# Linear attention and a gated feed-forward layer on one core: normed x of one superblock transposed by DMA, weights in three groups, a new order of all steps

## The chip, the cores and the metric

The kernel runs on one core of one Trainium2 chip. The metric is the device time of one execution in microseconds. Before the change three runs took 199.66, 199.82 and 200.43 us; the median is 199.82 us.

## What is computed

```
for t in range(768):                                  # per batch (4) and head (8), head size 48
    cur      = einsum('bhd,bhe->bhde', u * k[t], v[t])
    y[t]     = einsum('bhd,bhde->bhe', r[t], state + cur)
    state    = w[t] * state + einsum('bhd,bhe->bhde', k[t], v[t])
x  = y as 3072 tokens of 384
xn = x / sqrt(mean(x * x) + 1e-6) * rms_g
out = (silu(xn @ w_gate) * (xn @ w_val)) @ w_out      # 384 -> 1536 -> 384
```

r, k, v, w come as (4, 8, 768, 48) in float32, the weights in float32, and the output is (3072, 384) in float32.

## The kernel before

**Tiles.** Time is cut into six superblocks n of 128 steps, each with j = 0 to 3 for the batch: 128 tokens by 384 columns. A step of the program is written `name.n.j`. The recurrence becomes matmuls inside a superblock, with a running state `st` carried from one to the next.

**Attention steps of one tile.** `load_w`, `load_r`, `load_k`, `load_v` bring the inputs through SP's queue. `ln` (ScalarE) takes the logarithm of w, `cs_mm` (TensorE) sums it over time against a triangular mask, `cs_add` (DVE, superblocks 2 and up) makes the second sum, `exp_r` and `exp_k` (ScalarE) take the exponentials. `r_mul` (DVE) and `k_mul` (DVE in superblocks 0 and 1, GpSimd after) scale r and k into the tile `rk`. In superblock 1 the exponentials lie in SBUF (tiles `er`, `ek`), otherwise r's lie in PSUM. `rk` is transposed: by TensorE (`rk_pe`) and a ScalarE copy (`rk_tr`) in superblocks 0 and 1, by DMA from SP's queue (`rk_tr`) after. `q_mm` multiplies the transposed r and k into two PSUM banks; `q_mask_e` (DVE), `q_copy_o` (ScalarE) and `q_mask_o` (GpSimd, in superblock 0 DVE) mask them into `qts`. `cast_v` makes v bf16. `st_mm` and `st_new` make the next state. `bonus_mul` (two GpSimd multiplies, r by k and then by u), `bonus_sum` (DVE) and `bonus_v` (GpSimd) make the u term `ydiag`. `y_mm` puts the attention output in PSUM. `x_add` (DVE) adds `ydiag`; in superblock 0 TensorE adds it instead (`x_pe`).

**Norm.** `x_sq` (ScalarE) sums the squares, `x_rstd` makes the factor (GpSimd; ScalarE in superblock 0), `xn_mul` (ScalarE) writes the normed x in bf16. It is then transposed into `xnt`, in one of two ways. In superblocks 0 to 3: `xn_pe` (three TensorE transposes of 128x128 into one bank) and `xn_out` (DVE, a copy times the gain rms_g). In superblocks 4 and 5: `xn_tr` (a DMA transpose from SP's queue, L590), and after all four tiles `xn_gain`, three multiplies of 128x512 by the gain (L615 on DVE, L612 on ScalarE for one of them in superblock 4).

**Feed-forward.** For each superblock all four tiles go together, 512 tokens. `gate_mm.n.f` and `val_mm.n.f` (f = 0 to 11, L626, three matmuls each) fill two PSUM banks each in turn (rings `a`, tiles ps_au and ps_av, and `b`, ps_bu and ps_bv); `silu` (ScalarE) and `h_mul` (DVE) empty them into `ht`. `o_mm` (L672, twelve matmuls), `o_out` and `out_dma` give the output; they stand in the order when all twelve units of the superblock are done, between the attention steps of the next. `ln` and `exp` use one function table of ScalarE, `silu` another; `act` (L231) loads a table (L233) whenever the next function needs the other.

**Order.** The text ORDER lists every step. The program walks through it and calls the functions, so that each engine and each queue gets its instructions in that order; an engine runs on as far as its data and its place in its own list let it. `warm` steps are TensorE matmuls on zeros that nothing reads; 13 more stand ahead of everything. PSUM banks are dealt out by the same order: a step takes a bank whose last reader stands ahead of it. Weights are fetched on GpSimd's queue, which casts them: `load_gv.g.h` for the gate (h = 0) and value (h = 1) columns of group g, `load_wo` for the output weights. With GV = (0, 4, 12) group 0 holds the units f = 0 to 3 and group 1 the units 4 to 11.

**Start.** Ahead of the listed steps stand constants, a memset of the whole `st` (L313), and two TensorE broadcasts: u to all partitions (L333, copied by L334) and the gain as columns (L336, L337).

## Time and profile before

| what | us |
|---|---|
| median of three runs | 199.82 |
| span of the profiled execution | 199.4 |
| first feed-forward matmul starts | 31.30 |
| last matmul ends | about 196.4 |
| TensorE busy | 194.7 |
| DVE busy | 151.5 |
| ScalarE busy | 137.1 |
| GpSimd busy | 125.7 |

The span is from the first to the last instruction of one execution; the run times were taken in other executions, and their median is 0.42 us more. A row of the timeline gives the start, the duration, the engine, the line, the operation, the tiles and how many neighbouring instructions were merged, and in brackets the idle time of the engine before it with what released it. Matmuls overlap: a unit of three that lasts 0.81 us is followed by the next after 0.65 us.

### The profile page before, as it was taken

The numbers are of one execution on the slowest core, as the hardware profiler recorded it, in microseconds if no ns is written. First come the engines' busy times: TensorE is split into PE (matmuls) and PEld (weight loads), VectorE is DVE, ScalarE is ACT, GpSimd is POOL, SyncE is SP. The second block draws the span as 40 slices with busy tenths as digits, with TensorE's granted clock in tenths as the row PEclk, the third lists the DMA queues.
The fourth block names the chain that finished last, engine by engine and source line by source line (L and its number), as shares of the span: only waits on it lengthen the run. The fifth ranks groups of instructions, "written<-read, shape, count | busy, mean of one in ns | idle before, by whom it ended". The sixth has DMA issues, their size and how long they took to land.

```text
span 199.4 us, 4410 instructions
## 1 busy us (share of the span) xinstructions
PE 194.7 (98%) x1577; PEld 115.6 (58%) x1577; DVE 151.5 (76%) x290; ACT 137.1 (69%) x279; POOL 125.7 (63%) x184
## 2 busy tenths in 40 slices
PE   7999999999999999999999999999999999999994
PEld 3566666465765565665556665556555565555562
DVE  6157999799998799987889989987887873173611
ACT  3279998697998468968659959489886683164300
POOL 5369795099489777899857899967686861000000
PEclk9999999999999999999999999999999999999999
DMA  6999999999989999999989999986399012032012
GB/s 147 265 229 191 169 206 208 201 207 191 203 173 212 204 191 227 217 191 191 177 175 226 214 203 215 179 174 139 122 190 219 0 24 60 2 116 82 0 59 100
DMA packets 121566, 32.41 MB, mean 163 GB/s; under 512 B 116420, under 2 KB 120392, under 8 KB 121544
## 3 DMA queue, kind: packets, MB, share of 16 engines
q1 hardware_dynamic: 119504, 28.58, 67.8%
q0 software_dynamic: 2032, 3.54, 9.9%
q8 instruction: 12, 0.20, 0.4%
q14 instruction: 10, 0.08, 0.1%
q10 hardware_dynamic: 8, 0.00, 0.0%
HBM read 25.96 MB, written 4.72 MB: 154 GB/s over the span
## 4 chain that ended last, share of the span: by engine, by line
PE 88%; DMA 5%; DVE 2%; POOL 2%; issue 1%; ACT 0%
PE ps_bu L626 12%; PE ps_av L626 12%; PE ps_au L626 11%; PE ps_bv L626 11%; PE ps_qu L672 7%; PE ps_qz L672 7%; DMA wg_sb<-in_moe_w_gate_dram 5%; PE ps_qx L672 5%; PE ps_qv L672 5%; PE ps_qz L502 1%; PE ps_qx L552 1%; PE ps_qv L502 1%; PE ps_qv L333 1%; PE ps_qu L285 1%; PE ps_qu L502 1%
## 5 line engine op out<-in xcount | busy, mean ns | idle before, releaser
L672 PEld LDWEIGHTS <-ht 128*128 128x128 bf16 x300 | 28.2, 98 | 16.6
L626 PEld LDWEIGHTS <-wg_sb 128*128 128x128 bf16 x216 | 23.1, 114 | 19.8 <-DMA wg_sb<-in_moe_w_gate_dram 0.9
L626 PEld LDWEIGHTS <-wv_sb 128*128 128x128 bf16 x216 | 23.0, 114 | 18.3
L658 DVE TENSOR_TENSOR ht<-ps_bv,sg 128x512 bf16<-128x512 f32 x35 | 24.0, 687 | 10.2 <-PE ps_bv L626 9.1
L658 DVE TENSOR_TENSOR ht<-ps_bu,sg 128x512 bf16<-128x512 f32 x37 | 25.4, 687 | 6.9 <-PE ps_bu L626 5.8
L235 ACT ACTIVATE sg<-ps_av 128x512 bf16<-128x512 f32 x37 | 22.0, 596 | 12.2 <-PE ps_av L626 11.6
L626 PE MATMUL ps_av<-xnt,wg_sb 128*128 128x512 bf16 x111 | 30.1, 380 | 0.0
L626 PE MATMUL ps_bu<-xnt,wv_sb 128*128 128x512 bf16 x111 | 30.1, 380 | 0.0
L626 PE MATMUL ps_au<-xnt,wg_sb 128*128 128x512 bf16 x105 | 28.5, 380 | 0.5 <-DMA wg_sb<-in_moe_w_gate_dram 0.5
L626 PE MATMUL ps_bv<-xnt,wv_sb 128*128 128x512 bf16 x105 | 28.5, 380 | 0.0
L235 ACT ACTIVATE sg<-ps_au 128x512 bf16<-128x512 f32 x35 | 21.0, 600 | 10.5 <-PE ps_au L626 8.7
L467 POOL TENSOR_TENSOR ruk<-rt,kt 128x384 f32<-128x384 f32 x24 | 24.0, 1001 | 6.1 <-DMA kt<-in_k_dram 5.2
L468 POOL TENSOR_TENSOR ruk<-ruk,u_bc 128x384 f32<-128x384 f32 x24 | 24.7, 1030 | 1.9
L520 POOL TENSOR_SCALAR_AFFINE_SELECT qts<-qts 128x512 bf16<-128x512 bf16 x20 | 12.8, 650 | 15.1 <-ACT qts L513 14.6
L477 POOL TENSOR_TENSOR ydiag<-vt,diag 128x384 f32<-128x384 f32 x24 | 20.2, 843 | 1.7 <-DVE diag L472 1.6
L461 POOL TENSOR_TENSOR rk<-kt,ek 128x384 bf16<-128x384 f32 x16 | 15.9, 1004 | 2.3 <-ACT ek L235 2.3
L672 PE MATMUL ps_qu<-wo_sb,ht 128*128 128x384 bf16 (+1 forms) x96 | 15.0, 306 | 0.0
L672 PE MATMUL ps_qz<-wo_sb,ht 128*128 128x384 bf16 x84 | 14.8, 326 | 0.0
L233 ACT ACT_TABLE_LOAD x10 | 12.8, 1283 | 1.8 <-PEq L709 1.6
L472 DVE TENSOR_REDUCE diag<-ruk 128x8 f32<-128x384 f32 x24 | 13.0, 543 | 0.2 <-POOL ruk L468 0.2
L235 ACT ACTIVATE lw<-wt 128x384 bf16<-128x384 f32 (+1 forms) x20 | 11.1, 577 | 2.6 <-DMA wt<-in_w_dram 2.6
L585 ACT ACTIVATE xn<-xb,rstd 128x384 bf16<-128x384 f32 x20 | 11.8, 603 | 0.8 <-POOL rstd L580 0.7
(180 smaller groups left out, 379.8 us busy)
## 6 DMA issues: line engine op xcount, KB each, us to landing
rt<-in_r_dram SPq DMA_DIRECT2D x24, 192.0 KB, 4.0
kt<-in_k_dram SPq DMA_DIRECT2D x24, 192.0 KB, 4.2
vt<-in_v_dram SPq DMA_DIRECT2D x24, 192.0 KB, 4.0
out_dram<-ob SPq DMA_DIRECT2D x23, 192.0 KB, 2.3
wt<-in_w_dram SPq DMA_DIRECT2D x16, 192.0 KB, 4.0
wt<-in_w_dram SPq DMA_DIRECT2D x4, 384.0 KB, 4.4
wo_sb<-in_moe_w_out_dram POOLq DMA_DIRECT2D x3, 384.0 KB, 7.0
wg_sb<-in_moe_w_gate_dram POOLq DMA_DIRECT2D x1, 768.0 KB, 10.3
```

What stands on the lines that cost most here:

```text
L233: nc.scalar.preload_act_table_set(table_name)
L235: return nc.scalar.activation(**kw).ins
L461: eng.tensor_tensor(out=rk[:, n % 2, j, 1, :, 0:D], in0=inp["k", n, j], in1=bank["cs_k", n, j][:, 0:DM].rearrange("p (h d) -> p h d", h=H) ...
L467: nc.gpsimd.tensor_tensor(out=ruk[n, j], in0=inp["r", n, j], in1=inp["k", n, j], op=ALU.mult)
L468: nc.gpsimd.tensor_tensor(out=ruk[n, j], in0=ruk[n, j], in1=u_bc, op=ALU.mult)
L472: nc.vector.tensor_reduce(out=diag[n, j].rearrange("p h o -> p (h o)"), in_=ruk[n, j], axis=mybir.AxisListType.X, op=ALU.add)
L477: nc.gpsimd.tensor_tensor(out=ydiag[n, j], in0=inp["v", n, j], in1=diag[n, j].to_broadcast([128, H, D]), op=ALU.mult)
L520: nc.gpsimd.affine_select(out=qts[n, j][:, 1], in_=qts[n, j][:, 1], compare_op=ALU.is_gt, fill=0.0, base=0, pattern=[[0, NP], [1, 128]], c ...
L585: nc.scalar.activation(out=xn, in_=xb[n, j], func=AF.Copy, scale=rstd[n, j][:, 1, c:c + 1])
L626: nc.tensor.matmul(ps[:, cols], lhsT=units(ws, c, f), rhs=xnt[n][:, c, cols], start=(first and c == 0), stop=(c == KC - 1))
L658: nc.vector.tensor_tensor(out=ht[n][:, f, :], in0=bank.pop(("v", n, f)), in1=bank.pop(("sg", n, f)), op=ALU.mult)
L672: nc.tensor.matmul(ps[:, cols], lhsT=ht[n][:, f, b * L:(b + 1) * L], rhs=wo_sb[:, f, cols], start=(f == 0), stop=(f == FC - 1))
```

## The change

- X normed in superblock 3 is transposed by four `xn_tr` and multiplied by three `xn_gain`, in place of four `xn_pe` and four `xn_out`. The choice is made by which steps ORDER lists.
- GV = (0, 4, 8, 12): three groups of four units for gate and value, so six `load_gv` of equal size in place of two small and two large ones. They stand in the order 0.0, 0.1, 2.0, 1.0, 1.1, 2.1.
- `cast_v` of superblock 0 moves from ScalarE to GpSimd (CAST_ACT).
- The memset of `st` is dropped.
- The broadcasts of u and of the gain become steps (`u_mm`, `u_out`, `g_mm`, `g_out`). On TensorE they stay at the same place.
- The bonus product multiplies r by u first (`bonus_u`) and then by k.
- ORDER is new throughout. SP's first loads are now k, w, r, w, w, r, w, k, r, v, k, r, k, v, v (tiles 0.1, 0.1, 0.0, 0.0, 0.2, 0.1, 0.3, 0.0, 0.2, 0.0, 0.2, 0.3, 0.3, 0.1, 0.3); `ln.3.0` stands between SiLUs of superblock 1, and the last `y_mm` of superblock 5 directly ahead of the `o_mm` of superblock 4. The count of `warm` steps is 36 as before; one of them now follows the first `gate_mm`.
- PARTS and BEHIND are empty, so the functions that use them (`part`, `landed`) change nothing; `gate_h` and `val_h`, which no step used, are gone.

The core of the diff:

```diff
-    CAST_ACT = sel("00 01 02 03 10 11 12 13")
+    CAST_ACT = sel("10 11 12 13")
...
-    nc.vector.memset(st, 0.0)
...
-    u_ps = psum("q", None, [128, DM])
-    nc.tensor.matmul(u_ps, lhsT=ones_row, rhs=u_row, start=True, stop=True)
-    nc.vector.tensor_copy(out=u_bc.rearrange("p h d -> p (h d)"), in_=u_ps)
...
-    GV = (0, 4, 12)
+    GV = (0, 4, 8, 12)
...
+    def bonus_u(n, j):
+        ruk[n, j] = pt.tile([128, H, D], FP32, name="ruk", bufs=NRUK)
+        nc.gpsimd.tensor_tensor(out=ruk[n, j], in0=inp["r", n, j], in1=u_bc, op=ALU.mult)
+
     def bonus_mul(n, j):
-        ruk[n, j] = pt.tile([128, H, D], FP32, name="ruk", bufs=NRUK)
-        nc.gpsimd.tensor_tensor(out=ruk[n, j], in0=inp["r", n, j], in1=inp["k", n, j], op=ALU.mult)
-        nc.gpsimd.tensor_tensor(out=ruk[n, j], in0=ruk[n, j], in1=u_bc, op=ALU.mult)
+        if (n, j) not in ruk:
+            bonus_u(n, j)
+        nc.gpsimd.tensor_tensor(out=ruk[n, j], in0=ruk[n, j], in1=inp["k", n, j], op=ALU.mult)
```

From ORDER after the change, three places. Before the first `gate_mm`:

```
st_mm.0.3 cast_v.0.2 warm.6.0 warm.20.0 y_mm.0.2 r_mul.1.1 k_mul.1.1 bonus_mul.1.0 x_pe.0.3 y_mm.0.3 x_sq.0.2
x_rstd.0.0 xn_mul.0.0 st_mm.0.0 xn_pe.0.1 warm.15.0 load_gv.2.0 warm.16.0 st_new.0.0 load_gv.1.0 bonus_sum.1.0
...
xn_pe.0.3 warm.33.0 rk_tr.1.0 xn_out.0.3 r_mul.1.3 st_mm.0.1 cs_mm.1.2 exp_r.1.2 exp_k.1.2
bonus_mul.1.3 gate_mm.0.3 bonus_sum.1.1 k_mul.1.3 st_new.0.2 load_gv.2.1 warm.30.0 silu.0.3 val_mm.0.0 gate_mm.0.0
```

The norm of superblock 3:

```
o_mm.2.0 xn_mul.3.1 xn_tr.3.1 out_dma.1.2 x_rstd.3.2 x_sq.3.3 cs_add.4.0 load_r.5.0 st_new.3.3 x_rstd.3.3 exp_r.4.0
cs_mm.4.1 o_mm.2.2 cs_add.4.1 bonus_mul.4.2 exp_r.4.1 xn_mul.3.3 exp_k.4.1 exp_k.4.0 w_tot.4.0 r_mul.4.0 xn_mul.3.2
o_out.2.0 ln.4.2 xn_tr.3.3 xn_tr.3.2 w_tot.4.1 cs_mm.4.3 cs_add.4.3 k_mul.4.0 o_mm.2.1 bonus_sum.4.2 r_mul.4.1
st_mm.4.0 exp_r.4.3 k_mul.4.1 exp_k.4.3 w_tot.4.3 r_mul.4.3 bonus_mul.4.0 cs_mm.4.2 o_out.2.1 o_mm.2.3 cs_add.4.2
o_out.2.2 exp_r.4.2 out_dma.2.0 xn_gain.3.1 xn_gain.3.0 exp_k.4.2 rk_tr.4.1 rk_tr.4.0 k_mul.4.3 w_tot.4.2 xn_gain.3.2
```

The norm of superblock 5:

```
y_mm.5.2 x_rstd.5.1 val_mm.4.11 x_add.5.2 xn_mul.5.1 val_mm.4.6 h_mul.4.11 y_mm.5.3 h_mul.4.6 o_mm.4.3 x_add.5.3
x_sq.5.3 x_rstd.5.3 x_sq.5.2 o_mm.4.0 xn_tr.5.1 xn_tr.5.0 o_out.4.3 out_dma.4.3 x_rstd.5.2 xn_mul.5.3 xn_tr.5.3
xn_mul.5.2 o_mm.4.1 o_mm.4.2 xn_tr.5.2 xn_gain.5.2 xn_gain.5.1 xn_gain.5.0 gate_mm.5.2 val_mm.5.7 val_mm.5.2 o_out.4.1
```

More of the change, by code (lines that the diff above doesn't have):

```diff
@@ L86 @@
-h_mul.2.10 q_mask_o.3.3 bonus_sum.3.3 q_mask_o.3.2 cast_v.3.3 val_mm.2.11 xn_mul.3.0 q_mask_e.3.2 val_mm.2.9 silu.2.8
-h_mul.2.11 y_mm.3.2 st_mm.3.3 y_mm.3.3 load_r.4.2 ln.4.0 bonus_v.3.3 x_add.3.1 load_w.4.2 h_mul.2.9 val_mm.2.8
-x_add.3.3 cs_mm.4.0 bonus_mul.4.1 ln.4.1 cs_mm.4.1 x_sq.3.1 xn_pe.3.0 x_add.3.2 x_sq.3.2 cs_add.4.0 h_mul.2.8
-st_new.3.3 o_mm.2.0 x_sq.3.3 o_mm.2.2 exp_r.4.0 load_k.4.2 cs_add.4.1 exp_k.4.0 r_mul.4.0 x_rstd.3.1 xn_mul.3.1
-o_out.2.0 x_rstd.3.2 xn_mul.3.2 w_tot.4.0 ln.4.2 exp_r.4.1 load_r.5.1 x_rstd.3.3 k_mul.4.0 xn_out.3.0 load_r.4.3
```

272 lines of the change are left out of this document (135 added, 137 removed).

## Prediction, made before the changed kernel was run

> **What bounds the kernel now.** I read the page first, then the busy time by stage, then each engine's rows of the first 42 us. Page:
>
> ```profile
> span 199.4 us, 4410 instructions
> PE 194.7 (98%) x1577; PEld 115.6 (58%) x1577; DVE 151.5 (76%) x290; ACT 137.1 (69%) x279; POOL 125.7 (63%) x184
> ```
>
> Busy time by stage (PE, PEld, DVE, ACT, POOL, clock, DMA share, GB/s), cut where PE's first feed-forward matmul starts, where each superblock's first one starts, and where its last matmul ends:
>
> ```profile
> 31.30:196.43 165.13, 164.65 (x1323) 97.40 (x1320) 129.61 (x245) 114.37 (x230) 102.95 (x151) 1.00 0.75 156
> 196.43:199.39 2.96, 0.00 (x0) 0.00 (x0) 0.00 (x0) 0.32 (x1) 0.00 (x0) 1.00 0.29 102
> 31.30:62.08 30.78, 30.31 (x276) 18.47 (x274) 28.78 (x55) 25.86 (x52) 19.17 (x29) 1.00 1.04 200
> 90.66:119.27 28.61, 28.61 (x250) 17.17 (x248) 25.77 (x51) 21.39 (x44) 23.71 (x35) 1.00 0.98 198
> 146.83:173.05 26.22, 26.22 (x201) 15.05 (x200) 16.22 (x30) 15.27 (x32) 13.94 (x23) 1.00 0.38 77
> ```
>
> From 31.30 to 196.43 TensorE is packed: 0.48 us idle in 165.13, all in the first stage. The clock is full, so nothing off TensorE can shorten this part; it can only open gaps. The one gap, and the start of the part, stand in PE's rows:
>
> ```profile
> 31.30 0.81 PE L626 MATMUL ps_au<-xnt,wg_sb 128*128 128x512 bf16 x3
> 36.92 0.84 PE L626 MATMUL ps_au<-xnt,wg_sb 128*128 128x512 bf16 x3 [0.47 <-DMA wg_sb<-in_moe_w_gate_dram]
> ```
>
> It is the wait for the big second group of gate weights. The time therefore is a sum of four: start 31.30, matmuls 164.65, gaps 0.48, tail 2.96 = 199.39. I change each in turn. The profiled span is 199.4 where the median of the runs is 199.82; I add 0.42 at the end.
>
> **Matmuls.** Four `xn_pe.3` go. One costs PE its step to the next matmul, and the DVE copy `xn_out` goes with it; three `xn_gain` come on DVE:
>
> ```profile
> 27.39 0.33 PE L596 MATMUL ps_qu<-ident,xn 128*128 128x128 bf16 x3
> 27.56 0.33 PE L374 MATMUL ps_qv<-still 128*128 128x384 bf16 x1
> 30.61 0.54 DVE L607 TENSOR_TENSOR xnt<-ps_qv,gT 128x384 bf16<-128x384 bf16 x1
> 169.24 0.88 DVE L615 TENSOR_SCALAR xnt<-xnt,gT 128x512 bf16<-128x512 bf16 x3 [2.82 <-DMA xnt<-xn]
> ```
>
> 4 x 0.17 = 0.68 off PE (27.56 - 27.39). One `warm` of 0.16 now comes after the first `gate_mm`. Everything else after that step is the same set of matmuls: 164.65 - 0.68 + 0.16 = **164.13**. DVE saves 4 x 0.54 - 0.88 = 1.3 us in a stage where it has 2.8 us free (28.61 - 25.77); worth nothing to the end.
>
> **The start.** The first `gate_mm` needs `xn_out.0.3`, the last item of three queues. Removed first: the memset of `st`, and the casts from ScalarE.
>
> ```profile
> 3.25 1.34 DVE L313 MEMSET st<- 128x1536 uint32 x1 [0.27 <-issue]
> 7.00 0.56 DVE L334 COPY u_bc<-ps_qv 128x384 f32<-128x384 f32 x1 [2.41 <-PE ps_qv L333]
> L379 ACT CAST vb<-vt 128x384 bf16<-128x384 f32 x8 | 4.0, 509 | 0.0
> L381 POOL CAST vb<-vt 128x384 bf16<-128x384 f32 x16 | 8.0, 503 | 0.6 <-DMA vt<-in_v_dram 0.6
> ```
>
> The memset ends at 4.6, and DVE then waits 2.4 us for the broadcast of u: nothing gained. ScalarE sheds 4 x 0.51 = 2.0 us, GpSimd takes 4 x 0.50. GpSimd's rows of the start:
>
> ```profile
> 8.21 0.99 POOL L467 TENSOR_TENSOR ruk<-rt,kt 128x384 f32<-128x384 f32 x1 [4.39 <-DMA kt<-in_k_dram]
> 13.82 1.00 POOL L467 TENSOR_TENSOR ruk<-rt,kt 128x384 f32<-128x384 f32 x1 [0.92 <-DMA rt<-in_r_dram]
> 19.76 0.99 POOL L351 DMA_DIRECT2D wg_sb<-in_moe_w_gate_dram  x1
> 25.80 0.81 POOL L351 DMA_DIRECT2D wv_sb<-in_moe_w_val_dram  x1
> L468 POOL TENSOR_TENSOR ruk<-ruk,u_bc 128x384 f32<-128x384 f32 x24 | 24.7, 1030 | 1.9
> L477 POOL TENSOR_TENSOR ydiag<-vt,diag 128x384 f32<-128x384 f32 x24 | 20.2, 843 | 1.7 <-DVE diag L472 1.6
> ```
>
> The first multiply waits for SP's fifth load and the third pair for its tenth: (13.82 - 8.21)/5 = 1.1 us a load. In the new order it wants the sixth (r of 0.1), so it starts at about 9.3; that r comes before k lets the first of two multiplies run early does not change their sum. Up to the last cast GpSimd does four pairs (4 x 2.06), four casts (2.0), four `bonus_v` (3.4) and two weight issues (1.8): 15.4, so 24.7, plus about 0.8 for loads of v now issued later: 25.5. That cast gates `y_mm.0.2`, then the chain on ScalarE:
>
> ```profile
> 25.08 0.47 ACT L570 ACTIVATE junk<-ps_av 128x384 bf16<-128x384 f32 x1
> 28.45 0.58 ACT L585 ACTIVATE xn<-ps_bu,rstd 128x384 bf16<-128x384 f32 x1
> ```
>
> From this square to the last `xn_mul` it took 3.95 us for eight steps; the new queue has eight there too. 25.5 + 0.3 for the matmuls + 3.95 = 29.75. PE still has `xn_pe`, a warm, `st_mm` and `cs_mm.1.2` behind it (1.15): 30.9. So by GpSimd and ScalarE the start stays near 31. DVE decides:
>
> ```profile
> 24.91 1.35 DVE L455 TENSOR_TENSOR rk<-rt,er 128x384 bf16<-128x384 f32 x1
> 26.66 2.18 DVE L455 TENSOR_TENSOR rk<-rt,er 128x384 bf16<-128x384 f32 x1
> L455 DVE TENSOR_TENSOR rk<-rt,er 128x384 bf16<-128x384 f32 x4 | 4.7, 1184 | 0.0
> L461 DVE TENSOR_TENSOR rk<-kt,ek 128x384 bf16<-128x384 f32 x4 | 3.2, 807 | 0.0
> 20.71 0.69 DVE L509 TENSOR_TENSOR qts<-ps_qx,mask_lt 128x512 bf16<-128x512 f32 x1
> ```
>
> Multiplies with both inputs in SBUF (`er`, `ek`) are stretched, up to 2.18, where GpSimd is busy beside them. Ahead of `xn_out.0.3` there were three of them (two r, one k); now four (k of 1.1 too), and `bonus_sum.1.0`. The fourth bonus product leaves GpSimd at 9.3 + 11.7 = 21.0; from there DVE has 4 masks (0.69 each in the row, some 0.6 from start to start: 2.4), 2 sums and `w_tot` (1.0), 2 `st_new` (0.9), 4 `xn_out` (1.9) = 6.2, and the four multiplies. At the means 2 x 1.18 + 2 x 0.81 = 4.0 the queue ends at 31.2; with the two r as in this very stretch (1.35 + 2.18) and k at 0.81, 5.1, at 32.3. Below, PE's own matmuls of the start, 18.29 of 18.45 busy with their fillers, allow no more than about 1.4 off (to 29.9). I take **32.0**: the nearest rows are the two of this stretch.
>
> ```profile
> 12.85:31.30 18.45, 18.29 (x204) 11.86 (x203) 16.63 (x30) 16.85 (x42) 15.84 (x18) 1.00 1.06 194
> ```
>
> [...]
>
> **Gaps.** (a) Weights: six parts of equal size in GpSimd's queue instead of four. The first may stand at about 21.4 (19.76 before), the second at 24 (25.80 before), the third to fifth at 27.6 to 30; the order puts units of groups 1 and 2 after seven units of group 0 and an `rk_pe` (5.0 us), so at about 37. I take 0, with 0.5 as the upper end from the row at 36.92, and to -0.48 against before.
> (b) Between `rk_pe.1.2` and `q_mm.1.2` PE now has two feed-forward units and an `st_mm` (1.5) where it had three units and the `st_mm` (2.1). In that time ScalarE must reach and copy `rkT`:
>
> ```profile
> 62.72 0.65 PE ps_bu L626 x3
> 31.28 1.01 ACT L493 COPY rkT<-ps_qz 128x1024 bf16<-128x1024 bf16 x1
> ```
>
> With one SiLU (0.6) ahead of the copy it is 0.2 late; with none, nothing: 0.2.
> (c) `ln.3.0` now stands among the SiLUs of superblock 1, which adds two table loads:
>
> ```profile
> L233 ACT ACT_TABLE_LOAD x10 | 12.8, 1283 | 1.8 <-PEq L709 1.6
> L235 ACT ACTIVATE sg<-ps_av 128x512 bf16<-128x512 f32 x37 | 22.0, 596 | 12.2 <-PE ps_av L626 11.6
> ```
>
> Load, `ln` (0.5), load, SiLU: 3.7 us after `silu.1.4` until `gate_mm.1.8` gets its bank. From the end of `gate_mm.1.4` PE has five units of 0.65 and four small steps (1.1) before it: 4.35, against 0.8 (until `silu.1.4` is done) + 3.7 = 4.5: 0.2; nothing if ScalarE is early, up to 1 if late.
> (d) Superblock 3 now goes over SP:
>
> ```profile
> L590 SPq DMA_TRANSPOSE xnt<-xn x8: 1177/1200/1605, 134.8 to 166.8; - x8
> xnt<-xn SPq DMA_TRANSPOSE x8, 2.3
> rkT<-rk SPq DMA_TRANSPOSE x16, 3.4
> 165.25 1.95 PE ps_qz L672 x12
> 163.96 0.55 DVE L561 TENSOR_TENSOR xb<-ps_qx,ydiag 128x384 f32<-128x384 f32 x1
> ```
>
> SP issues one in 1.2 us, it lands 2.3 us after. PE covers with four `o_mm` of 1.95 and three small steps, 8.8 us. The last `xn_mul.3.2` stands on ScalarE behind `exp_r.4.1`, which needs `cs_mm.4.1` (6.6 before PE is free) and a DVE add, so it starts 5.8 before; three `exp` and two `xn_mul` follow (0.4 and 0.55 from start to start), so `xn_mul.3.2` ends 3.5 before; 2.3 + 0.88 leave 0.3. But DMA's share there is 0.98, not 0.38 as where the eight ran; with 3.4 it is 0.8 late. The four also hold SP's loads of superblock 5 behind them, which have 5 us and more in hand. I take 0.4.
> (e) Superblock 5: its last `y_mm` moved from before 11 us of PE work to before 7.8 (the four `o_mm`). From `x_add` at 163.96 to the end of the gains at 170.12 the chain took 6.2; a second square, an output copy and the 1.2 us of the transpose ahead are new in it: about 8.0: 0.2.
> Gaps: 0 + 0.2 + 0.2 + 0.4 + 0.2 = **1.0**.
>
> **Sum.** 32.0 + 164.13 + 1.0 + 2.96 (same tail: half-width copy and one output) = 200.1; with 0.42, **200.5**, 0.35% above the median. About 0.5%, 1.0 us, is what a measurement of this kernel tells from no change.
>
> **Rivals.** *Faster:* the order is simply tight everywhere. Start 30.2, gaps 0.1: 30.2 + 164.13 + 0.1 + 2.96 + 0.42 = 197.8. For it: before, hundreds of steps ran with 0.48 of gaps, and ScalarE has 2 us less at the start. Against: GpSimd starts later and has more. *Slower, by the lock:* all four multiplies wait for a GpSimd instruction (r at 2.18 as at 26.66, k at 0.55, an undisturbed pass of this size, plus 1.0: 2 x 2.18 + 2 x 1.55 = 7.5 instead of 5.1): start 32.0 + 2.4 = 34.4, time 202.9; it decides as soon as the four take over 5.5 in sum, because nothing else on DVE gives. For it: GpSimd has no idle time beside them now. Against: the k rows' mean of 0.81. *Slower, superblock 3:* the transposes land behind loads on SP's queue (3.4 plus one load's 1.1 instead of 2.3): 1.7 late instead of 0.4, and 0.4 at superblock 4, whose stage has 2.5 us more GpSimd work by my count of the order: 202.2. For it: the DMA share of 0.98; against: SP stands waiting for `xn_mul.3.1` just before, so that few loads are under way.
>
> **Chances.** Forecast 0.48, its own range 199.3 to 201.8 (start 31.2 to 32.7, gaps 0.6 to 1.6; of it 0.30 within 0.5%, 0.16 above, 0.02 below), faster 0.22, lock 0.15, superblock 3 0.15. So faster 0.24, same 0.30, slower 0.46. The range leaves out the far end of each: 198.0 (faster rival, 197.8, with a little of its gap) to 203.0 (the lock).
>
> **What would show it.** In the new profile: first feed-forward matmul at 32 (30 for the faster rival, 34 for the lock, then with r and k multiplies of over 1.5 us); PE idle 1 us after it, at the places (b) to (e) by name of releaser: DVE `xnt` for superblocks 3 and 5, ACT `sg` for the table loads; 12 table loads. The prediction is wrong if PE shows idle time at a place I do not name, or if its matmul total after the start isn't 0.5 us smaller.

## The result and the profile after

The changed kernel takes 212.83 us (median of four runs, 210.22 to 213.08) where the kernel before takes 199.78. The ratio is 1.0588, 95% interval 1.0518 to 1.0659. Ratios here and below leave out executions that took over 1.5% longer than the fastest of their kernel, which the medians still count, so a ratio can differ from the quotient of two medians. The forecast was 200.5 us with 203.0 as its upper end, so the loss was missed by 12 us. On a second chip the changed kernel, run again unaltered, gave 1.0715 (1.0673 to 1.0756). So a difference of about 1% between runs on different chips says little, and below the stages of the profiles are compared beside the ratios.

The page of the kernel after: span, busy times and the granted TensorE clock in 40 slices.

```profile
span 211.1 us, 4349 instructions
PE 195.1 (92%) x1544; PEld 114.6 (54%) x1565; DVE 148.9 (71%) x288; ACT 140.0 (66%) x277; POOL 128.1 (61%) x190
PEclk9999996999999999999999996999999999999999
```

TensorE's busy time is much as before (194.7), its share fell from 98% to 92%: most of what was added is idle time. Two slices have a lowered clock, at 32 to 37 and at 127 to 132 us. The busy time by stretch (PE, PEld, DVE, ACT, POOL, granted clock, DMA share, GB/s), cut at the steps of the forecast and around those two slices:

```profile
30.14:35.08 4.94, 4.82 (x33) 3.25 (x33) 2.36 (x5) 1.62 (x4) 4.76 (x6) 0.66 1.24 211
36.33:207.70 171.37, 165.69 (x1289) 97.10 (x1308) 128.17 (x242) 117.96 (x232) 101.22 (x149) 0.99 0.72 146
207.70:211.10 3.40, 0.03 (x1) 0.00 (x0) 0.00 (x0) 0.32 (x1) 0.00 (x0) 1.00 0.18 61
124.60:127.06 2.46, 0.19 (x2) 0.00 (x0) 1.70 (x4) 1.10 (x1) 2.38 (x4) 1.00 0.71 190
127.06:131.10 4.04, 3.37 (x12) 1.43 (x14) 2.12 (x5) 1.56 (x3) 2.84 (x3) 0.58 1.14 148
```

The first feed-forward matmul starts at 36.33, the last matmul ends at 207.70. Put against the terms of the forecast (the profiled run itself took 212.78):

| term | forecast | measured | difference |
|---|---|---|---|
| start | 32.0 | 36.33 | +4.3 |
| matmuls and gaps after it | 164.13 + 1.0 | 171.37 | +6.2 |
| tail | 2.96 | 3.40 | +0.4 |
| time minus span | 0.42 | 1.68 | +1.3 |

The last line is no part of the kernel's work: the run times of before exceed its spans by 1.7 us too wherever both come from one execution (202.52 beside a span of 200.8 on the chip of the first experiments); by that, an estimate, the profiled execution of before was some 1.3 us above the median run, which adding 0.42 hid. The two that matter are the start and the gaps.

**The start.** PE's first matmuls of `y_mm.0.2`, which wait for the last cast of v on GpSimd, its first step after its idle stretch, and its first feed-forward unit; then VectorE's rows there:

```profile
25.97 0.36 PE L560 MATMUL ps_av<-vb,qts 128*128 128x48 bf16 x8 [0.76 <-POOL vb L385]
30.14 0.33 PE L604 MATMUL ps_qv<-ident,xn 128*128 128x128 bf16 x3 [1.62 <-ACT rstd L237]
36.33 0.81 PE L634 MATMUL ps_au<-xnt,wg_sb 128*128 128x512 bf16 x2
```

```profile
24.21 0.58 DVE L465 TENSOR_TENSOR rk<-kt,ek 128x384 bf16<-128x384 f32 x1
27.47 0.89 DVE L459 TENSOR_TENSOR rk<-rt,er 128x384 bf16<-128x384 f32 x1 [2.68 <-ACT rstd L237]
28.29 1.34 DVE L465 TENSOR_TENSOR rk<-kt,ek 128x384 bf16<-128x384 f32 x1
29.55 0.54 DVE L545 TENSOR_TENSOR st<-ps_qv,wcol 128x384 bf16<-128x384 f32 x1
33.50 0.56 DVE L615 TENSOR_TENSOR xnt<-ps_qu,gT 128x384 bf16<-128x384 bf16 x1 [1.56 <-PE ps_qu L604]
35.32 0.56 DVE L615 TENSOR_TENSOR xnt<-ps_qx,gT 128x384 bf16<-128x384 bf16 x1 [1.26 <-PE ps_qx L604]
```

VectorE stands for 2.68 us ahead of `r_mul.1.1`. The releaser that is named, a tiny ScalarE step, writes nothing that this multiply reads. Its r is loaded by the later of these two issues on SP:

```profile
L253 SPq DMA_DIRECT2D rt<-in_r_dram x2: 704/984/1264, 19.6 to 20.9; - x2
DMA to landing us min/median/max: 4.0/5.2/6.5
```

Issued at 20.9, landed 6.5 us later: 27.4. (That the longer landing belongs to the later issue is inferred here; a row of the order alone, below, names the load.) Behind the multiply come `k_mul.1.1` and `st_new.0.0` (29.55, L545), and `st_new.0.0` frees the PSUM bank ps_qv that `xn_pe.0.0` needs: PE goes on at 30.14, right after it. PE was idle for 1.62 us, and from here to 35.08 its clock is 0.66 in the mean; one matmul of 128x384 follows another after 0.32 us instead of 0.16. The last two `xn_out` then wait for PE, not PE for them. From 25.97 PE needs 7.04 us for its own list up to the first unit when nothing holds it, as two runs below show: 25.97 + 7.04 + 1.62 of idle time + 1.7 of half rate = 36.33.

**Superblock 3.** SP's rows, then VectorE's gains, then PE:

```profile
120.29 0.53 SPq L690 DMA_DIRECT2D out_dram<-ob  x1
120.87 0.42 SPq L253 DMA_DIRECT2D rt<-in_r_dram  x1
121.38 2.64 SPq L598 DMA_TRANSPOSE xnt<-xn  x2
```

```profile
125.36 1.64 DVE L623 TENSOR_SCALAR xnt<-xnt,gT 128x512 bf16<-128x512 bf16 x2 [1.48 <-DMA xnt<-xn]
127.00 1.08 DVE L623 TENSOR_SCALAR xnt<-xnt,gT 128x512 bf16<-128x512 bf16 x1
```

```profile
127.06 0.41 PE L634 MATMUL ps_av<-xnt,wg_sb 128*128 128x512 bf16 x1 [2.27 <-DVE xnt L623]
128.14 0.59 PE L634 MATMUL ps_av<-xnt,wg_sb 128*128 128x512 bf16 x1 [0.67 <-DVE xnt L623]
128.60 1.47 PE L634 MATMUL ps_au<-xnt,wg_sb 128*128 128x512 bf16 x3
```

The last two transposes are issued at 121.38 and about 122.7, behind an output and a load; the later one lands near 125.3; a gain takes 0.82 and 1.08 us; PE is idle 2.27 us, starts its first unit, waits 0.67 for the third gain, and runs at half rate: a unit lasts 1.47 instead of 0.81. In the profile before, four of VectorE's five gains took 0.35 us; the fifth, one of these two at superblock 4, took 1.09, beside a GpSimd multiply:

```profile
145.22 1.35 DVE L615 TENSOR_SCALAR xnt<-xnt,gT 128x512 bf16<-128x512 bf16 x2
```

**Two smaller places.** An output copy (L682) that waits for an output transfer, which SP issued at 94.28, keeps `h_mul` and with it PE:

```profile
98.71 0.56 DVE L682 COPY ob<-ps_qu 128x384 f32<-128x384 f32 x1 [1.85 <-DMA out_dram<-ob]
100.38 0.81 PE L634 MATMUL ps_bv<-xnt,wv_sb 128*128 128x512 bf16 x3 [0.62 <-DVE ht L660]
155.40 1.96 DVE L623 TENSOR_SCALAR xnt<-xnt,gT 128x512 bf16<-128x512 bf16 x2 [0.31 <-DMA xnt<-xn]
157.41 0.62 PE L634 MATMUL ps_bu<-xnt,wv_sb 128*128 128x512 bf16 x2 [0.81 <-DVE xnt L623]
```

The lower two rows are superblock 4, whose gains are stretched as well. The gaps after the start add up to 171.37 - 164.13 = 7.2 us: 4.4 at superblock 3 (2.4 until its first matmul, 0.9 at the third gain, 1.1 of half rate), 1.3 at superblock 4, 0.8 at 99.6, and some 0.7 in small pieces.

### The profile page after: what moved, and what is told of

Read it like the earlier page. It is cut to its first block, busy times and chain, and to the rows that moved or that the text cites. A ratio compares the mean times of both kernels' runs of the same rounds, so it can differ in the third digit from the quotient of the medians.

```text
span 211.1 us, 4349 instructions
## 1 busy us (share of the span) xinstructions
PE 195.1 (92%) x1544; PEld 114.6 (54%) x1565; DVE 148.9 (71%) x288; ACT 140.0 (66%) x277; POOL 128.1 (61%) x190
## 4 chain that ended last, share of the span: by engine, by line
PE 68%; SPq 8%; DMA 7%; ACT 5%; POOL 5%; DVE 3%; issue 2%; DVEq 0%; ACTq 0%; POOLq 0%
PE ps_au L634 11%; PE ps_bv L634 10%; PE ps_av L634 10%; PE ps_bu L634 9%; SPq L253 6%; PE ps_qx L675 6%; PE ps_qv L675 4%; PE ps_qu L675 3%; PE ps_qz L675 3%; DMA out_dram<-ob 2%; SPq L266 2%; DMA rkT<-rk 2%; DMA rt<-in_r_dram 2%; POOL rk L465 1%; DVE xnt L623 1%
## 5 line engine op out<-in xcount | busy, mean ns | idle before, releaser
L237 ACT ACTIVATE sg<-ps_av 128x512 bf16<-128x512 f32 x35 | 20.9, 598 | 20.1 <-PE ps_av L634 18.4
L660 DVE TENSOR_TENSOR ht<-ps_bu,sg 128x512 bf16<-128x512 f32 x35 | 24.0, 686 | 13.9 <-PE ps_bu L634 8.9
L634 PE MATMUL ps_av<-xnt,wg_sb 128*128 128x512 bf16 x101 | 28.5, 382 | 3.2 <-DVE xnt L623 2.9
L634 PE MATMUL ps_au<-xnt,wg_sb 128*128 128x512 bf16 x109 | 30.6, 387 | 0.3
L660 DVE TENSOR_TENSOR ht<-ps_bv,sg 128x512 bf16<-128x512 f32 x37 | 25.4, 685 | 6.8 <-PE ps_bv L634 3.6
L634 PE MATMUL ps_bu<-xnt,wv_sb 128*128 128x512 bf16 x99 | 28.3, 383 | 1.1 <-DVE xnt L623 0.8
L471 POOL TENSOR_TENSOR ruk<-rt,u_bc 128x384 f32<-128x384 f32 x24 | 24.1, 1003 | 5.6 <-DMA rt<-in_r_dram 5.6
L476 POOL TENSOR_TENSOR ruk<-ruk,kt 128x384 f32<-128x384 f32 x24 | 24.0, 999 | 4.3 <-DMA kt<-in_k_dram 2.6
L675 PE MATMUL ps_qx<-wo_sb,ht 128*128 128x384 bf16 x96 | 16.9, 326 | 0.0
L578 ACT ACTIVATE junk<-xb 128x384 bf16<-128x384 f32 x20 | 10.3, 516 | 5.7 <-DVE xb L569 5.6
L675 PE MATMUL ps_qu<-wo_sb,ht 128*128 128x384 bf16 (+1 forms) x84 | 13.8, 314 | 0.0
```

The costliest lines, as they stand in the source:

```text
L237: return nc.scalar.activation(**kw).ins
L471: nc.gpsimd.tensor_tensor(out=ruk[n, j], in0=inp["r", n, j], in1=u_bc, op=ALU.mult)
L476: nc.gpsimd.tensor_tensor(out=ruk[n, j], in0=ruk[n, j], in1=inp["k", n, j], op=ALU.mult)
L634: nc.tensor.matmul(ps[:, cols], lhsT=units(ws, c, f), rhs=xnt[n][:, c, cols], start=(c == 0), stop=(c == KC - 1))
L660: nc.vector.tensor_tensor(out=ht[n][:, c, cols], in0=bank.pop(("v", n, f))[:, cols], in1=bank.pop(("sg", n, f))[:, cols], op=ALU.mult)
L675: nc.tensor.matmul(ps[:, cols], lhsT=ht[n][:, f, b * L:(b + 1) * L], rhs=wo_sb[:, f, cols], start=(f == 0), stop=(f == FC - 1))
```

## Experiments

The theory after the result had three parts: the late load of r.1.1 holds VectorE, and PE through a bank; the path over DMA costs about 5 us at superblock 3; an idle stretch of PE brings a lowered clock, which doubles its price (1.62 us idle and 1.7 of half rate at the start). The rivals were the lock between VectorE and GpSimd at the start, the gains (not the transposes) at superblock 3, and the new order itself rather than the three named parts. The lock is the prediction's name for a supposition, that a VectorE multiply with both inputs in SBUF waits for a GpSimd instruction to end; shown is that in the profile before the four `r_mul` with both inputs in SBUF took 0.55 to 2.18 us, the two of 1.35 and 2.18 beside GpSimd's work, and the 20 with one input in PSUM 0.54 to 0.56. In the diffs of steps below, a line is a part of ORDER cut to the steps that move.

### The start: the load of r.1.1 earlier

```diff
-warm.1.0 load_r.1.1 rk_pe.0.3
+q_mm.0.1 load_r.1.1 load_k.1.0
```

> The kernel after with one step moved: the load of r for superblock 1, batch 1 is SP's 17th load instead of its 21st. Late-load theory: r_mul.1.1 stood idle 2.68 us on VectorE because this r, issued at 20.9, landed at 27.4; st_new.0.0 behind it held the bank that xn_pe.0.0 needs. With the load early r_mul.1.1 starts at about 24.8, st_new.0.0 at 27.5, TensorE is not idle 1.62 us at 28.5, and the first feed-forward matmul stands at 32.3 to 33 instead of 36.33: 3.3 to 4 us faster, about 209.2. Rival, the VectorE/GpSimd lock of the prediction: the multiplies start earlier but are stretched beside GpSimd (over 1.5 us each), st_new.0.0 still starts at 29, first feed-forward matmul at 35.5 or later: within 1 us of the kernel after.

Measured 215.11 us, ratio 1.0662 (1.0594 to 1.0730); first feed-forward matmul at 35.42. VectorE:

```profile
26.46 2.58 DVE L459 TENSOR_TENSOR rk<-rt,er 128x384 bf16<-128x384 f32 x1
28.97 1.35 DVE L465 TENSOR_TENSOR rk<-kt,ek 128x384 bf16<-128x384 f32 x1
```

The wait is gone, so it had been the load; but the multiply, now beside GpSimd's work (90% busy or more from 26.7 to 32.0 on this run's page), lasts 2.58 instead of 0.89 and ends at 29.04, later than the 28.4 of the changed kernel. The theory that the late load costs the time by itself fell: when the load comes early, the stretched multiply takes its place. The load that moved up also held others back: `r_mul.1.0` waited 1.07 us for its r (0.18 before the move), and `y_mm.0.2` began at 27.72 instead of 25.97. PE is idle there for 0.56 us instead of 1.62 and keeps its clock; less the later `y_mm.0.2`, that is the 0.9 us of the start. Superblock 3 took it back: PE was idle there for 4.51 us, and the clock was low for nearly 7:

```profile
127.00:134.00 7.00, 5.67 (x17) 2.04 (x18) 5.04 (x10) 1.56 (x3) 3.13 (x4) 0.51 0.95 196
```

### The start: both multiplies behind the last xn_out

```diff
-y_mm.0.2 r_mul.1.1 k_mul.1.1 bonus_mul.1.0
+y_mm.0.2 bonus_mul.1.0
...
-xn_out.0.3 r_mul.1.3
+xn_out.0.3 r_mul.1.1 k_mul.1.1 r_mul.1.3
```

> The kernel after with r_mul.1.1 and k_mul.1.1 moved on VectorE from ahead of st_new.0.0 to behind xn_out.0.3; nothing else. Theory after the run with the early load (r_mul.1.1 then started at 26.46 and took 2.58 us, k_mul.1.1 1.35): these two, late for their data or held by GpSimd, are what keeps the bank of st_new.0.0 from xn_pe.0.0. Behind the last xn_out they cost nothing: st_new.0.0 at 27.5 to 28.5, no idle 1.6 us of TensorE, first feed-forward matmul 32.2 to 33.5 (36.33 in the kernel after with half clock, 35.83 in one like it without), the kernel 2.5 to 4 us faster, ratio to before 1.040 to 1.046. Rival: GpSimd's queue (last cast of v at 25.4 to 27, then the chain on ScalarE) sets the start anyway: first matmul at 35 or later, under 1 us won.

Measured 212.73 us, ratio 1.0543 (1.0481 to 1.0604); first feed-forward matmul at 33.29. VectorE, then PE from `y_mm.0.2` on:

```profile
32.76 1.40 DVE L459 TENSOR_TENSOR rk<-rt,er 128x384 bf16<-128x384 f32 x1
34.08 1.35 DVE L465 TENSOR_TENSOR rk<-kt,ek 128x384 bf16<-128x384 f32 x1
```

```profile
26.25 0.36 PE L560 MATMUL ps_av<-vb,qts 128*128 128x48 bf16 x8
38.88 0.81 PE L634 MATMUL ps_bv<-xnt,wv_sb 128*128 128x512 bf16 x3 [0.93 <-DVE ht L660]
```

The idle time ahead of `xn_pe.0.0` is gone and so is the half rate: from 26.25 to 33.29 PE goes through its list in 7.04 us (7.03 in the mended version below). So the two steps ahead of the norm are what made PE stand there. How much that is worth varies: six profiles with the start of the changed kernel unaltered have their first unit at 34.83 to 37.34, so 33.29 is 1.5 to 4.1 us earlier (3.0 against the first of them). But at their new place the multiplies keep `h_mul` of superblock 0, and PE waits 0.93; the stage up to the first `o_mm` took 22.46 instead of 21.38 us. Superblock 3 idled 3.25 us here, and in the median little was won.

### The start: twelve more warm matmuls

```diff
+warm.16.0 warm.40.0 ... warm.51.0 st_new.0.0
```

> The kernel after with twelve more filler matmuls (0.16 us each) on TensorE ahead of xn_pe.0.0, where it stands idle 1.62 us at 28.5. Idle-time theory of the clock: the half clock granted from 30.5 to 35.1 follows from that idle time; filled, the 4.9 us of work after it take about half, the first feed-forward matmul stands at 33.9 and the kernel is 2.4 us faster, about 210.4. Rival: the clock falls for the idle time spread from 10 to 28 us or for something that is not idle time; then nothing changes, or 0.3 us are lost.

Measured 217.02 us, ratio 1.0761 (1.0694 to 1.0829). PE is not idle there and the clock stays full, as the idle-time theory wants, but no time could be won: PE's row of the fillers, three old and twelve new, shows why.

```profile
29.04 5.62 PE L378 MATMUL ps_qx<-still 128*128 128x384 bf16 x15
```

All write one bank and follow each other after 0.36 us, as the three on one bank in the changed kernel do (1.08 in sum at 27.44), not 0.16 as those on changing banks do (7.67, 7.83 and 7.99 there), so `xn_pe.0.0` comes at 34.50, 2.6 us after the bank was free. Inconclusive, by the fault of the experiment.

### Superblock 3: back to TensorE, two ways

```diff
-xn_tr.3.0 ... xn_tr.3.1 ... xn_tr.3.3 xn_tr.3.2 ... xn_gain.3.1 xn_gain.3.0 ... xn_gain.3.2
+h_mul.2.8 xn_pe.3.0 xn_out.3.0 o_mm.2.0
+k_mul.4.0 xn_pe.3.1 xn_out.3.1 o_mm.2.1 xn_pe.3.3 xn_out.3.3 xn_pe.3.2 xn_out.3.2 bonus_sum.4.2 r_mul.4.1
```

> The kernel after with the named part undone alone: superblock 3's normed x goes through TensorE again (xn_pe and xn_out for the four batches, no transposes by DMA and no gains; st_mm.4.0 goes behind them for want of a bank). Theory that the DMA path is what opens the boundary of superblock 3: the 4.4 us lost from the end of the last o_mm of superblock 2 (124.63) on, idle and half clock, go, four times 0.17 of matmuls come back: 3.5 us faster, about 209.3. Rival, that the last xn_mul on ScalarE (ended 121.1) or the new order around it is late anyway: TensorE still stands over 1 us before the first feed-forward matmul of superblock 3 and less than 2 us are won.

Measured 212.07 us, ratio 1.0524 (1.0462 to 1.0586). In this first trial I had put `xn_out.3.3` and `xn_out.3.2` ahead of `r_mul.4.1` on VectorE, and PE waited 1.87 us behind them. The second trial spreads them:

```diff
+h_mul.2.8 xn_pe.3.0 xn_out.3.0 o_mm.2.0
+cs_mm.4.1 xn_pe.3.1 xn_out.3.1 o_mm.2.2
+k_mul.4.0 xn_pe.3.3 xn_out.3.3 o_mm.2.1 xn_pe.3.2 bonus_sum.4.2
+o_out.2.2 xn_out.3.2 exp_r.4.2
```

> The kernel after with superblock 3's normed x on TensorE again, the copies placed on VectorE where their inputs are just ready (in the first trial of this, two of them stood ahead of r_mul.4.1 and made TensorE wait 1.87 us themselves). Theory that the DMA path opens the boundary: TensorE goes from the last o_mm of superblock 2 to the first matmul of superblock 3 with under 0.4 us idle, no half clock there; 4.4 us of loss go, 0.7 of matmuls come back: 3 to 3.7 us faster than the kernel after, ratio to before 1.040 to 1.044. Rival: the last xn_mul or the masks and copies on VectorE are late in this order too: over 1 us idle stays and under 2 us are won.

Measured 208.79 us, ratio 1.0325 (1.0234 to 1.0417), with the last kernel of this study the lowest in the new order, 3.9 us below the run of the moved multiplies on the same chip. From the first `o_mm.2` to superblock 3's first unit:

```profile
115.29:124.85 9.56, 9.54 (x79) 6.10 (x77) 8.94 (x22) 7.37 (x19) 8.07 (x13) 1.00 0.82 192
```

No idle time, clock 1.00; in the changed kernel this stage took 11.19 us (115.87 to 127.06), and the feed-forward behind it 21.09 where it is 19.14 here. That makes 3.6 us for the path over DMA by the stages of these two profiles; by the two ratios, from different chips, it is 5.3.

### Superblock 3: the transposes ahead on SP's queue

```diff
-xn_tr.3.1 out_dma.1.2 x_rstd.3.2 x_sq.3.3 cs_add.4.0 load_r.5.0 st_new.3.3
+xn_tr.3.1 x_rstd.3.2 x_sq.3.3 cs_add.4.0 st_new.3.3
...
-xn_tr.3.3 xn_tr.3.2 w_tot.4.1
+xn_tr.3.3 xn_tr.3.2 out_dma.1.2 load_r.5.0 w_tot.4.1
```

> The kernel after with out_dma.1.2 and load_r.5.0 moved behind the last transpose of superblock 3 on SP's queue. Theory: those two keep the third transpose until 121.38 though its input was ready at 119.9, and the fourth until 122.7. Without them the third goes at 120.3, the fourth at 121.5, the gains start 1.2 us earlier: 1.2 us faster (211.6) if TensorE still falls to half clock, 2.3 us (210.5) if the shorter idle time keeps the clock. Rival: GpSimd's instructions, not the landing, set the end of the gains: under 0.5 us.

Measured 212.97 us, ratio 1.0535 (1.0439 to 1.0632). SP, then VectorE:

```profile
119.72 3.80 SPq L598 DMA_TRANSPOSE xnt<-xn  x3
123.61 0.53 SPq L690 DMA_DIRECT2D out_dram<-ob  x1
```

```profile
125.78 0.56 DVE L682 COPY ob<-ps_qz 128x384 f32<-128x384 f32 x1 [2.58 <-DMA out_dram<-ob]
126.25 1.51 DVE L623 TENSOR_SCALAR xnt<-xnt,gT 128x512 bf16<-128x512 bf16 x2
```

The last two transposes go out some 0.4 us earlier, but now the output transfer is late; VectorE's output copy waits 2.58 us for its buffer, and the gains stand behind that copy. PE was idle 3.25 us. One wait was exchanged for another: what was put behind the transposes became the late one.

### Superblock 3: less GpSimd work beside the gains

This kernel leaves out the bonus products of three tiles, so it does not compute the same output; it serves to see the gains with GpSimd idle.

```diff
+    LEAN = sel("40 43 53")
...
+        if (n, j) in LEAN:
+            nc.gpsimd.tensor_copy(out=ruk[n, j][:, :, 0:1], in_=inp["r", n, j][:, :, 0:1])
+            return
         nc.gpsimd.tensor_tensor(out=ruk[n, j], in0=inp["r", n, j], in1=u_bc, op=ALU.mult)
```

> The kernel after without the two multiplies of the bonus on GpSimd for three blocks (superblock 4, batches 0 and 3; superblock 5, batch 3), and their sums cut to one column: so GpSimd has little or nothing to do while VectorE applies the gains of superblock 3. Lock theory: a gain took 0.82, 0.82 and 1.08 us there because it waited for GpSimd's instruction to end; now 0.35 each, the first feed-forward matmul of superblock 3 comes 0.9 us and the second 1.6 us earlier: 1.6 to 2.5 us faster (with or without the half clock). Rival: the gains are slow because transposes are landing in the same tile or for their own sake: durations unchanged, time within 0.5 us.

Measured 214.10 us, ratio 1.0535 (1.0469 to 1.0602). SP, then VectorE:

```profile
123.46 2.65 SPq L604 DMA_TRANSPOSE xnt<-xn  x2
```

```profile
129.06 0.61 DVE L629 TENSOR_SCALAR xnt<-xnt,gT 128x512 bf16<-128x512 bf16 x2 [3.95 <-DMA xnt<-xn]
129.66 0.34 DVE L629 TENSOR_SCALAR xnt<-xnt,gT 128x512 bf16<-128x512 bf16 x1
```

With GpSimd idle beside them (its last step ended at 126.57) the gains run in 0.34 to 0.35 us from one to the next, where they took 0.82 and 1.08 in the changed kernel beside GpSimd multiplies (one after the other from 122.82 to 129.90): their stretch goes with GpSimd's work, as the lock theory expected. No time was won. In the execution that was profiled (215.50 us) the transposes were issued 2.1 us later than in the changed kernel, 1.0 of it because the whole stage stood later, and took some 4 us to land, so that with the gains cheap the transposes alone made PE wait 3.98 us; whether the other executions went the same way, no profile shows. So the gains need not be the cause for PE to stand, and the rival that they alone are falls.

### The named parts one by one, in the old order

```diff
-    CAST_ACT = sel("00 01 02 03 10 11 12 13")
+    CAST_ACT = sel("10 11 12 13")
```

> The kernel before, its old order kept, with one part of the change: v of superblock 0 cast on GpSimd instead of ScalarE. Theory: GpSimd, which was idle only some 2 us between 12 and 24 us, gets 2.0 us more, its last product for superblock 0 and the casts come up to 2 us later than the matmuls that want them, so the start grows by 0.5 to 2 us: 200.5 to 202. Rival (the prediction's sum: GpSimd's queue with the casts still ends in time): start within 0.3 us, the same time.

```diff
-    GV = (0, 4, 12)
+    GV = (0, 4, 8, 12)
...
-load_gv.0.1 load_gv.1.0 ... bonus_sum.1.1 load_gv.1.1
+load_gv.0.1 load_gv.2.0 load_gv.1.0 ... bonus_sum.1.1 load_gv.2.1 load_gv.1.1
```

> The kernel before with one part of the change: gate and value weights in three groups of four units, the third group issued ahead of the second (its units come first in the old order). Theory: the half-sized parts land earlier, the one wait of 0.47 us for the gate weights at 36.9 goes: 0.3 to 0.5 us faster. Rival: all parts share the same engines, the part that is wanted lands no earlier, and two more issues on GpSimd (0.8 us each) push its products back: the same or up to 0.8 us slower.

```diff
-xn_pe.3.0 ... xn_out.3.0 ... xn_pe.3.1 xn_out.3.1 ... xn_pe.3.3 ... xn_pe.3.2 ... xn_out.3.3 ... xn_out.3.2
+xn_mul.3.0 xn_tr.3.0 ... xn_mul.3.1 xn_tr.3.1 ... xn_mul.3.2 xn_tr.3.2 ... xn_mul.3.3 xn_tr.3.3
+exp_r.4.3 xn_gain.3.1 xn_gain.3.0 xn_gain.3.2 cs_add.4.2
```

> The kernel before, its old order kept, with the named part of the change alone: normed x of superblock 3 transposed by DMA, each transpose right behind its xn_mul in the queues, three gains on VectorE where the last copy stood. Theory: the last xn_mul there ends at 115.5, a transpose takes 1.2 us of SP and 2.3 to 4.2 us to land, and two gains beside a busy GpSimd take 1.6: first feed-forward matmul of superblock 3 at 121 to 123 instead of 119.3, and half clock for 3.4 us after an idle stretch of that length: 2 to 5 us slower. Rival, the prediction's own: 0.4 us late, 0.7 us of matmuls saved: the same time.

The casts alone: 202.36 us, 1.0058 (1.0028 to 1.0088). The three groups alone: 202.44, 1.0046 (1.0011 to 1.0081). The DMA path alone: 208.07, 1.0303 (1.0237 to 1.0369). PE's waits that the first two add, one row of the casts and one of the groups:

```profile
32.73 0.40 PE L484 MATMUL ps_qv<-ident,rk 128*128 128x128 bf16 x4 [0.69 <-DVE rk L461]
```

```profile
42.09 0.84 PE L626 MATMUL ps_bv<-xnt,wv_sb 128*128 128x512 bf16 x3 [1.73 <-DMA wv_sb<-in_moe_w_val_dram]
```

Both are small: a wait just behind the first unit, which itself came no later (31.00, where up to 2 us more were expected), and one for the value weights of the group that now stands third. The DMA path alone, SP, VectorE and PE:

```profile
120.56 1.18 SPq L590 DMA_TRANSPOSE xnt<-xn  x1
```

```profile
123.56 2.43 DVE L615 TENSOR_SCALAR xnt<-xnt,gT 128x512 bf16<-128x512 bf16 x3 [2.15 <-DMA out_dram<-ob]
```

```profile
124.97 0.41 PE L626 MATMUL ps_bv<-xnt,wv_sb 128*128 128x512 bf16 x1 [3.92 <-DVE xnt L615]
```

The same picture as in the changed kernel, in another order of steps: last transpose behind loads and an output, gains of 0.8 us each, 3.92 us of idle time, then half rate (granted clock 0.50 from 126 to 129). (A gain reads no output; the transfer that the row names can't have released it, while the transpose issued at 120.56 lands in about that time, by the 2.3 to 3.0 us that one took in the profile before.) From the first `o_mm.2` to the first `o_mm.3` it took 34.05 us where the kernel before took 27.93, so this is the largest of the named parts, 6 us. (The profiled execution, 209.81 us and the longest of its four, also waited 2.19 and 0.89 us for weights at 35.05 and 39.37, ahead of everything that was changed; that is no cost of the DMA path.)

### The new order without the named parts, and the changed kernel again

```diff
-    CAST_ACT = sel("10 11 12 13")
+    CAST_ACT = sel("00 01 02 03 10 11 12 13")
...
-    GV = (0, 4, 8, 12)
+    GV = (0, 4, 12)
```

with superblock 3 over TensorE as in the second way above.

> The kernel after with all three named parts undone and only the new order of the steps kept: superblock 3 through TensorE (as in the second trial of that), v of superblock 0 cast on ScalarE, weights in two groups. If the parts add up (on the old order alone the casts cost 0.58%, the groups 0.46%, superblock 3 by DMA 3.03%): ratio to before 1.0325 of the second trial less 1.0%, about 1.022, so that the order itself costs some 4.5 us, most of it ahead of the first feed-forward matmul (35.6 in the second trial). Rival, that the order is only as late as the named parts make it: ratio under 1.010, first feed-forward matmul under 32.5.

> The kernel after, unchanged, once more on the chip of this comparison: ratio to before 1.052 to 1.066 as first measured. The half clock should be granted after each stretch of over 1.9 us without a matmul and after none under 1.5 us; the one of 1.6 to 1.8 us before xn_pe.0.0 may go either way.

On one chip: the order alone 209.65 us, 1.0417 (1.0385 to 1.0449); the changed kernel 215.08, 1.0715 (1.0673 to 1.0756). So the order carries somewhat more than half of the loss, and the named parts in it 5.4 us. The expectation, 1.022, was far too low: by the product of their ratios the three parts cost 4.1% in the old order, the new order without them costs 4.2%, and all of it costs 7.2%, so the costs are not a plain sum (the old-order runs are from another chip). "The order" here includes what this run keeps: the dropped memset, the two broadcasts as steps and the bonus product in its new form, which no run tries by themselves. VectorE, PE and the clock at the start of the order alone:

```profile
28.26 0.57 DVE L459 TENSOR_TENSOR rk<-rt,er 128x384 bf16<-128x384 f32 x1 [2.56 <-DMA rt<-in_r_dram]
30.62 0.33 PE L604 MATMUL ps_qv<-ident,xn 128*128 128x128 bf16 x3 [1.76 <-DVE st L545]
36.74 0.81 PE L634 MATMUL ps_au<-xnt,wg_sb 128*128 128x512 bf16 x2
```

```profile
31.00:34.60 3.60, 3.49 (x17) 1.80 (x16) 1.42 (x4) 1.02 (x3) 2.94 (x3) 0.53 1.20 230
```

Without any cast moved and with the old weight groups the start is still 36.74, and here the profile names the load and the step that I had inferred, `st_new` (L545). Stage by stage this kernel's profile (span 208.3) lies 8.9 us above that of before: 5.4 at the start, 1.0 in the feed-forward of superblock 2 (the output copy), 0.7 and 0.9 at the change to superblocks 3 and 4, and under 0.4 anywhere else.

The second profile of the changed kernel (span 211.2) has the same steps and another cause at the start. VectorE waits for no load there; its multiplies are stretched instead, the first two of four:

```profile
22.69 1.68 DVE L459 TENSOR_TENSOR rk<-rt,er 128x384 bf16<-128x384 f32 x1
26.09 1.09 DVE L465 TENSOR_TENSOR rk<-kt,ek 128x384 bf16<-128x384 f32 x1
```

With 1.35 and 1.34 for the other two they sum to 5.46, and `st_new.0.0` begins at 29.64, where with the late load it began at 29.55. PE was idle for 1.07 us, the clock did not fall, and the first unit stands at 34.83. Of the six profiles with this start two show the late load and four the stretched multiplies (5.46 to 5.69 in sum).

### Without fillers, and a mended version

In the kernel before, the last 15 `warm` steps ahead of its first feed-forward unit are left out:

```diff
-warm.17.0 ... warm.25.0 ... warm.20.0 ... warm.6.0 warm.35.0 ... warm.15.0 ... warm.23.0 ... warm.3.0 warm.16.0
-warm.0.0 ... warm.30.0 ... warm.14.0 ... warm.28.0 warm.33.0 ... warm.11.0
```

> The kernel before without the last fifteen of its filler matmuls (from warm.17.0 on, in TensorE's queue between 21 and 31 us): 2.4 us of idle time in short pieces, none over 1.2 us. If the clock goes by the sum of idle time over some microseconds, half clock is granted near 30 us, costing up to 1.7 us: 201.5. If it takes one unbroken stretch of about 1.6 us or more, as before each fall seen so far, the clock stays full and the time is that of the kernel before within 0.5 us, or 0.3 better where a filler stood in the way.

Measured 201.18 us, 1.0020 (0.9983 to 1.0056): no difference. PE's idle pieces, none over 0.56 us where the fillers had stood, the longest 0.84 at the weights at 36.98, did not lower the clock, which stayed at 1.00 over the start.

Last, the repairs together on the changed kernel: superblock 3 over TensorE, the two multiplies late, the output transfer earlier, and one pair of bonus multiplies behind the last `x_rstd` of superblock 4:

```diff
-y_mm.0.2 r_mul.1.1 k_mul.1.1 bonus_mul.1.0
+xn_out.0.3 r_mul.1.1 k_mul.1.1 r_mul.1.3
-xn_mul.2.3 out_dma.1.1 k_mul.3.1
+o_out.1.1 out_dma.1.1 bonus_mul.3.0
-xn_mul.4.1 bonus_mul.5.1 cs_add.5.2
+x_rstd.4.3 bonus_mul.5.1 r_mul.5.1
```

> The kernel after with four of its places mended together: superblock 3 through TensorE as in the second trial; r_mul.1.1 and k_mul.1.1 behind xn_out.0.3; out_dma.1.1 right behind o_out.1.1 on SP; bonus_mul.5.1 behind x_rstd.4.3 on GpSimd (it kept the last normed x of superblock 4 back by 2 us). If the losses are these and add up: 5.3 us (second trial) + 1 to 2.5 (start) + 0.8 (output buffer) + 1 (superblock 4) off the kernel after, ratio to before 1.010 to 1.020. Rival: each mended wait lets another one through, and the ratio stays at 1.03 of the second trial.

Measured 208.42 us, 1.0324 (1.0259 to 1.0389), no better than superblock 3 over TensorE by itself. The start came to 34.54 and the wait of the output copy is gone, but PE waits 0.89 us for `h_mul` at 40.08, and at superblock 4:

```profile
150.91 2.11 DVE L623 TENSOR_SCALAR xnt<-xnt,gT 128x512 bf16<-128x512 bf16 x2
```

The gains there take 1.05 us each, no less than in the second trial (0.97) and in the changed kernel (0.98); in all three, two bonus multiplies of GpSimd stand beside them. So moving one pair did not free the gains, and PE still waits 1.04 us at 153.07. No kernel of this study beats the one before.

## Why the prediction was wrong

**What held.** The matmul total after the start, as far as it can be read: what PE's busy time (165.69) has over 164.13 is about what the half rate at superblock 3 adds. GpSimd's queue at the start: its last cast ended at 25.92, forecast 25.5. Gap (a), the weights: nothing. Gap (c): twelve table loads, 0.26 us lost, forecast 0.2. Gap (e): 0.18, forecast 0.2. The place of `xn_mul.3.2` in (d): it ended 3.5 us before PE was free, as worked out.

**The failed step: the start, 32.0.** Two terms of its sum failed. The first is VectorE's work, where every instruction of the queue counted as runnable when its turn came and only the length of the multiplies was bounded. In the profiled run they lasted less than in the sum: 0.56, 0.58, 0.89 and 1.34, together 3.4 instead of 5.1. What was left out is what `r_mul.1.1` waits for: its load stands 21st on SP's queue now, and 2.68 us went there. Left out too is what stands behind it: `st_new.0.0` holds the bank of `xn_pe.0.0`, so a stall of VectorE became one of PE, 1.62 us, and half rate followed, 1.7 us more. The second term is TensorE's own list, which entered only as a floor of 29.9. Behind the first matmul of `y_mm.0.2` PE has 7.04 us of work, eleven `warm` steps among it that take about 3; the sum put 5.4 us from the last cast (25.5) to the start on the way over ScalarE (30.9). With the forecast's own cast the list alone gives over 32.5. It measured 25.97 + 7.04 = 33.0, 1.0 above the forecast; 1.62 and 1.7 make up the 4.3. Moving the two multiplies took the idle time and the half rate away twice (33.29 and 34.54), so that place is shown; no run takes fillers out of the new list.

The lock rival (34.4) was not what held VectorE in the first profile, since the four took less than its point of decision, 5.5. Its term, that each of the four waits for a GpSimd instruction, 7.5 us in sum, is shown by no run; what the two profiles of the changed kernel show in its place is 3.4 and 5.46. But stretched multiplies are what held VectorE in the second of them, and in three more with that start; GpSimd was busy for 90% or more from 21.1 to 31.7 there, but no run takes that work away at the start. The late load and the stretch stand in for each other from one execution to the next, and the theory after the result, made from one profile, took one for the cause and the other for its rival. Both had to be in the sum, as the later of the two. That 34.4 lies near the 34.83 of the second profile is in part luck: that time is made of a `y_mm.0.2` at 26.61, the list and 1.07 us of idle time.

Beside GpSimd's work such a multiply took up to 2.58 us, against 0.55, and a gain 0.82 to 1.08 against 0.35. I had reckoned with a stretch for the multiplies and not for the gains.

**The failed step: gap (d), 0.4.** Its sum was 2.3 for the landing and 0.88 for the gains after `xn_mul.3.2`, 3.2 of the 3.5 us there were. Measured from the same point: 1.6 until the second of the two transposes could be issued (the output, the load and the other transpose are ahead of it), 2.6 to land, 1.64 for the two gains that the first matmul needs: 5.9, so 2.4 late. Then 0.9 for the third gain and 1.1 for the clock: 4.4. The rival for superblock 3 had the place and a smaller price, 1.7 (its own terms, 3.4 + 1.1 + 0.88 - 3.5, give 1.9); it lacked the stretched gains and the clock. I had read the gain from a stage with GpSimd quiet (0.29 each, in 0.88 for three), though the same change put it into a stage with four GpSimd multiplies beside it, and the gain of 1.09 stood in the profile before.

**Places not named.** The output copy at 98.71 (0.8) and superblock 4 (1.3). My own test said that idle time at an unnamed place makes the prediction wrong; it does. Both come from the order, as the order alone shows them too, and I had counted superblock 4 only within the rival.

**What was not counted at all** is that waits are dear here: of the 11.7 us that the start (36.33 instead of 31.30) and the gaps (7.2 instead of 0.48) cost, about 2.8 are half rate after idle time. And the order was costed step by step at the five places where I expected trouble; by the run with the order alone it costs about 4%, with none of the named parts.

**What stays open.** Why the transposes were issued and landed later in some runs than in others (issue from 119.72 to 123.46, landing 2.3 to some 4 us) is not settled, nor why the load of r.1.1 is late in some executions only, nor why the same kernel differs by 1.3% between two chips.
